# A new table of orders, engines and PSUM banks for a four-layer attention kernel on one core

## The chip, the core and the metric

The kernel runs on one core of a Trainium2 chip. A core has five engines that run side by side, each with its own instruction stream that it works off in order: TensorE (PE: matmuls, with its weight loads shown apart as PEld), VectorE (DVE), ScalarE (ACT), GpSimd (POOL), and SyncE (SP), which here only issues DMAs. PE writes its results to PSUM, a memory of eight banks per partition; DVE and ACT read them from there and write to SBUF, the working memory. The engines wait for each other by semaphores.

The metric is the device time of one execution in microseconds (us). Before the change it is 412.26 us, the median of three runs (411.99 to 412.7).

## The reference

The input x has 2048 rows (tokens) of 512 numbers in bf16. Four layers follow each other, each of the form x = x + attention(layernorm(x)), with 32 heads of 16 numbers: a linear attention (A), a sliding attention (B), A again and B again, with the same weights for both A and for both B.

```python
def _A_ref(x, wqkv, wo):            # linear attention
    phi = lambda t: jnp.where(t > 0, t + 1, jnp.exp(t)) + 1e-6
    pq, pk = phi(q), phi(k)
    kv = jnp.einsum("bhsd,bhse->bhde", pk, v)
    z = jnp.einsum("bhsd->bhd", pk)
    num = jnp.einsum("bhqd,bhde->bhqe", pq, kv)
    den = jnp.einsum("bhqd,bhd->bhq", pq, z)[..., None] + 1e-6
    o = num / den                   # then o @ wo
...
def _B_ref(x, wqkv, wo):            # each row sees itself and the 255 rows before it
    scores = jnp.einsum("bhqd,bhkd->bhqk", q, k) * (Dh ** -0.5)
    mask = (idx[:, None] - idx[None, :] >= 0) & (idx[:, None] - idx[None, :] < W)
    p = _softmax(jnp.where(mask[None, None], scores, -1e9), axis=-1)
    o = jnp.einsum("bhqk,bhkd->bhqd", p, v)     # then o @ wo
```

## The kernel before

**Tiles and stages.** The rows are cut into 16 tiles of 128. The program first builds a graph of 2559 operations (class Plan), each a small group of instructions on one engine, with what each must wait for. The stages are:

1. The first A layer's keys (layer_a_keys): for each tile a layer norm (norm: statistics L374 and L375 on DVE, two tiny steps L379 and L380 on POOL, the normalised tile L381 on DVE), a transpose of the tile (a DMA, L389, or PE with a copy, L395 and L402), key and query projections (tok L420, feat L434) and the function phi (exponential L444 on ACT, the rest L446 to L451 on ACT and DVE). A product of normalised input and keys is summed over all tiles (L501).
2. The barrier: the summed product becomes a small matrix M; denominators are formed (L563, L569) and spread (L579), and the queries are divided (L589, L591).
3. The first sliding layer (middle(2)). For each tile: the output of the A layer (tok L420), the residual (L604, DVE), a norm, a transpose, the B projections (feat L434, tok L420), and copies of their results out of PSUM: queries by "bqe" (L407), keys by "bke" (L627 on ACT, L628 on DVE) and values by "bve" (L407). A DMA spreads the keys ("kd", L636) and one the values ("vd", L655). Then the scores (L676, and L792 for the far end of the window), their exponentials "ex" on ACT (L686, L801), the masks of the near triangle on DVE (L694) and of the far triangle ("mf") on DVE (L773) or on POOL (L772), the product with the values (L822), the division (L834, L835), a transposing DMA (L389) and the output projection with its residual. As each tile ends, the next A layer's norm, keys and values (their copy is "ve", L407) are begun.
4. The second barrier, then the second sliding layer (middle(3)), whose finished tiles are sent to the output by DMAs ("outp", L942), issued by SP or POOL.

**Which operations have a choice.** Most operations are bound to one engine. Copies out of PSUM (made by copy, either and transpose) may run on ACT or on DVE; a far mask on DVE or POOL; an output DMA on SP or POOL.

**What sets the order.** Nothing is scheduled while the kernel is built. A packed string, TABLE (from L954), holds a decision for everything, and place (L92) reads it: two bytes for each of the 2559 places give the operation that stands there in one overall order; one byte for each operation gives its engine; one byte for each of the 1005 PSUM tiles gives its bank, 0 to 7. Each engine then runs its own operations in that overall order.

```python
order = [ops[raw[2 * k] + 256 * raw[2 * k + 1]] for k in range(n)]
o.eng = ("PE", "ACT", "DVE", "POOL", "SP")[raw[2 * n + o.i]]
x.banks = [raw[3 * n + k]]
```

Two waits follow from the table itself. A PSUM tile that takes over a bank waits until the tile that held the bank before has been read. And a long POOL operation (a far mask among them) is made to wait for the nearest short DVE operation (norm or mask) that stands before it in the overall order. synchronise (L133) turns all dependencies into semaphore waits; SP's DMAs use a ring of 48 semaphores.

Of the kernel before, what the change touches and what calls it, by code (L numbers as in the profile page):

```python
# [11 lines left out]
P = 128  # L12
D = 512
DH = 16
S = 2048
T = 16
# [219 lines left out]
class Plan:  # L236
# [715 lines left out]


TABLE = (  # L954
    r"c-qZZ1GH_+j;*AUO4YS(+qP}nwr$(CZQHhO+h*^z&%Lkz@5lf8{~o>0SxP0TnVDHN_6n(#3ZYPu0>vt{(khG!tBeY#;;UdPxccG}D67J&gzBTqtRkpSE~5J8",
    r"5~(cegG;Qksun7VilmaNY^tS-tg@?Cs*n2YqNp6IwMwQYsGKUfimLi5QE62hl|uDX(NtR%N~Ke|RXdeZEmn<GdevXmRuk0{HA!Vqb<_a0O)XUeRbACyrBahs",
    r"V>L)^R~^(cHAU4^JJeJaL)BLuRT{NZEmtvBF_lrRP@U9ZwM)fPomF&oOYK&%RYR3Y4N<q%3Ds5IQA1TX6;}mT2I8o@s=Lag;;Cuso@$~}tCMP&y050IH|msX",
    r"sv4-_YKA(kR;rn5l{%y5s#)r+TCEDIE=r(>daH`7HEN#9t0F*8wMPX~7J8`>s)SmrMk)ur)hP8&1%ml1BJ5SURA4BhvcMd*PmNZIV1b&g_N(_QE38usRV4VJ",
    r"&Zz_HqlygYRdrPi8o&khKqZDKkOYduLv>L_g>2AFtyh=SBb84bRF72<$PQ0bP$&VHRSpOSC84>>2~X7+6&yaPr0`jdQ)5*rIHbO)WY7?j!&emzzNxAzI$Tj9",
    r"pftpQ{OXyC2?}CC1(ge&8n1Fg5S0Q7sXUMp@<J#`1^J+`Dg$L9HGEfPRT>xvjUXhHgE$aW6;S0N9aMnvPyi}H5!D!KLu_aYwP2A-3sqEps0c+>JE#FQVS}ou",  # L960
    r"+Cv?v3-zF!st+BY2^?0Pp@wP$9iauZg;vlKHmWYr3|hkx)d`wIcX+Ojs;{mGOn|O%OihI2YLlw0UZ_d1SzT2x)k4^!CPO8)2(GCq&<&=-3D~L@!*$gYrol;=",
    r"4mZ>$SOV45W>^X{;1mEXgPCwsAuNZvumUvnf_bnKN~&2<Ud@Lsa2RT-*{}e%!V#DQ+n_g`hNG|@*1{{*57xnP*a0_TJ?w;4&<A$GYUm5MU=5rBf{?fYUaPZk",
    r"8%kqMbqxB$J=h4Lkl_K8!E+EAOR3OsAI`%wD2o>$47`BdP!9J%SO|l6VIMq)aBv6q!(NDm2Ounlhqn+8W8*srj~Ah|ii4NnJw(8`_y{h;6?g&%p*&uNhfo0{",
    r";sAII*B~)g#DQ=gli~$D1eLH3Cc%qX8RO$qsEY}3EY`ytFb)&q2e=NYaXfy6PmmVlVS4xs8K6FXfi!pttKdtxjIUq<W`rx49wT7}oQSXCDrSPnI0=(sReS>(",
    r"aWY21sE8O16Ja&X3=OdXCdcU52&>~YOo5GY3bw^eI2CJPI&6<AaUQ0^`B)R%p~mY-xB#0XV`glQ9WV<Te1OgHD+p%AhiEYyeurt82Opus>G%zrU`GsuG4Te@",
    r"z|MFR17i!U47acoDy#y4*)cEH#vGUrYhg>wiTSY=7Qh%-6&7O`j0;OKH_pUrFbiAb608onFbEdJpx6eN;c_g5!EiR-#+7&ngJWTg2SqRhuE3($74Kp<j1Q}D",
    r"J$A<guo@TPMob86um^6yemDr$;yN4*n{gp-#i39Pi{lX3f)VvFh@>}R34Dp$@HLji?N|zT;46%*zhV?!O@G7cdMEC}{`ehh=mYo^qv`=zQ$NROx*!b1Cs+ug",
    r">t`54_ryUMQzz1e;RVjtz3>gr(SxxFJkYgtQK+qZV`BXnhu~cOP$$ttu@8R4gZK%D;URpahhtwH4xjNb?nb5O;#=H<BcP7HkMD3Ve!)4ITG!R@5%dvEtM?=7",
    r"4_Hs9(T{a<y$@sQCtB;2I<_W#4@Y1e{Zt3iDfCE8r=RJ}dY&GIjdW6-MaR{naSX=OS@nE<6tnA8`WQCW@pTTJUN_Olae>aDbLxe<jb5ZP>iW8^&ZHaY6PQc4",
    r"(<iZmey#)SY`UTDsDtQaI=61GgX&J2bsil|8{J$7*Ligd-C2jwqVwq<x}`3nd+9aW>QmTLC(urx#>KjiK7(s@Kix&I(;;<h-BtJ1p>!*K7B}i{`W%MVn{`p$",  # L970
    r"T^G~+^(Nh0Z`H;10G&{8(<Ssky<L~o`SliEN)OV@byGc97tkwoY28dO(Pi{Xy+Ie$d-YPiUw_nv^)g*nf71K(NC=}x>QV4nht;DYoIa>u=&_KL4(ntTUXOu7",
    r"x|}|w*XsznyiQIP^bkEt57ia*OI=C7(!+EL8m)KellrwzNn>;?N=2u1YdWG+(@uRrpVnz;mmaRu(pZf&Lch^OZD_TAt9R?8dX*lhHMOPj`k3CM-{}eZtp29c",
    r"(Q&P4qFzrY^dx;oZ=mlw5N)LNbWR5*pp2A(GEop>`l5r;CNlIvhoGP&)Q;Zk%+#KOQ*QdI&+87<k@C_7ZE3Q06q54L6n#-=qwF+QU()%h6HU{h=&~+A)Abb{",
    r"nsU%pU64vs7|KasC@htwuT+R4Q$FfOW$2pjPTwdO6{o^fj!M#Xy_tGY5!yl}XaH@cqSTp+(LgFiUFbWNr$MB+D-EFvG?cc{4PB9L>S0ugYEU>jK(}-h3QxCn",
# [12 lines left out]
    r"gp}$MN-{}$$swVohD4Bvl1rvbO_?D%rHRaxVUk&z$#BUc;bnw0l{_+1vPxbVCAB1*jF#GxUGm8oDI#MflH``6GEO2(9Z6w|Nfb$Gl1hGQA*oDVDIo=<rKC0m",
    r"C5<UAt)zn_lR}c+6qZhs!<3Xs(oyP}dNNt+o5qsKOp!(=vuPwbO+(W~vX};@lysBQlFMW@xy^X#DifrP?30O-&CHSRvR~#&b2%@a<$@fLxza~2N)PEP2c@U<",
    r"lS49J7RX^~E#IV<ER^rkTaHK@IV#F7l4H`?tdJ(At*n%(lFoviC9C9$w3DdPUea5%S7os@vjauj)zaK%umj|ptdZH0(Jqm-(!wqkvZrL7uw5p`-jL;TT3Xs$",
    r"a$L^H3ArijWs9`3*JXp8lh$^doRp0+P1@M4@<1-jCJAmg%R}ieA?zTzBq8l187ybzi3}03&m@z*ErD!i+tyn9R31wf8^&g}fo(YJY&LsGo=aGJSAy6bvQr}1",  # L990
    r"d-6i=OGJCuyp%|GyVS9v?JLP|UrSvZ%0{*YY<Anu7PR&38wqc7*tfDvg4vvQx4e@$c8^4{L2X?7UiL~<`%ykfE*sBAvjc2yJIJ=Td29ze&_=g0Y)9MO#<V@`",
    r"Cy8Zy+9dX~<g>|aY}?6xk<K=$jc<$CE;fNJW(V7Zwy14t3fn|BvHdE|ObOfEl(O^eeA~jLv?c8VTftVcrR{ZF$hI`=ZC+c^F0_5@4ZFzpv&HQOyV%~eDQsW6",
    r"(N?jk>@8c>ma+Zq5?j_*vr}w2o7yh5Q|)bA-Y&Bd+#Q?7Ms(BcU0dDmv6XEkx7XINk=;H!#@@3vZE`!#F1NMp3R~NbwNYF{JHoECQQZ*Rz>c)5?0vi1j<P%K",
    r"8avePwDoOC*V|6FyX+R*%MP={Z7H|auC@E^c)QJZwMXn|+sKx7M{PGd!#1{M+&cTh9<v{9S=YqAwB_7q``Es+<=rQ{+n%t|+;%&`Hnk`11v}B6vYYKB`_>+}",
    r"lkF4x-p;h|>{IL90UOvwcL(ir8_2OcWMjAo_OKOq+CH>r>?Zrj8u!(Hu^;SN`_0a>=j?3z-JZ8W+$EdM&9Mnx4rg5=H`l(gF<o|-*u`?Mt#YYcZ1>EjcFA0F",
    r"7ssV=aa|gh&c$<=ZF(2VU9q)X1((5HwG~}1SKFm^*KA6c+ks2q>Ns?HTt*ktHFiN=Q>R@a7tA$r?Okw3E`;mgs=B-`r>o{J+K#TitL`efX0D;D=?c4{(!e!$",
    r"p<P+2>{_}^u8NEATDZ<Gv#a5{xO^_D%i^-SB(AG#<wm<kF25V&!nnGwfD7viy0NaFo9@E7nXZ!??!vonu85oA2D!m5tsUuBxgl<Z8}G)s)o!9|?bf&nu8o`R",
    r"+PYD$yPM-?xgM^ao9iaI&2E_M=_b2gZmXN;`noA@iQD4VyQyxP+u(+}`EHx*;}*D$uD9Fo*1CnRs5|Huxnk~s+wGRR;;x_D<2JeeZo6CT*0}+0ue<0DxgBnx",
# [168 lines left out]
```

## Time and profile before

| | |
|---|---|
| median of 3 runs | 412.26 us (411.99 to 412.7) |
| span of the profiled execution, first to last instruction | 410.8 us |
| granted TensorE clock | 1.000 |
| matmuls, weight loads | 7668, 7742 |
| DVE, ACT, POOL instructions | 807, 448, 216 |
| DMA traffic | 37.19 MB, most of it inside the chip; HBM read 6.29 MB, written 2.10 MB |

The profile is of one execution. Its span leaves out what lies before the first and after the last instruction; the median of the runs is 1.5 us above the span, and this difference is carried along unchanged in all sums. An engine's "busy" is the time in which at least one of its instructions runs. Matmul ends are modelled, so PE's busy share is not its share of useful work. A line like L420 is shared by several steps, since helpers record it.

### The profile page before, as it was taken

How to read it: one execution, taken by the hardware profiler on the slowest of the kernel's cores; microseconds unless marked ns; L12 is line 12 of the kernel's file. 1: busy time of each engine (PE TensorE's matmuls, PEld its weight loads, DVE VectorE, ACT ScalarE, POOL GpSimd, SP SyncE). 2: the span in 40 equal slices, each digit the busy share in tenths (PEclk: the TensorE clock that was granted, in tenths of full speed). 3: DMA queues.
4: the chain of work that ended last, by engine and by line, in shares of the span. 5: the costliest groups of instructions: out<-in, count | busy, mean ns of one | idle time of the engine just before them, and what ended most of it. 6: DMA issues, size and time to landing. Idle time of an engine off the chain costs nothing.

```text
span 410.8 us, 17540 instructions
## 1 busy us (share of the span) xinstructions
PE 386.9 (94%) x7668; PEld 260.3 (63%) x7742; DVE 344.5 (84%) x807; ACT 352.8 (86%) x448; POOL 122.4 (30%) x216
## 2 busy tenths in 40 slices
PE   7999999999999999999999999999999988999896
PEld 3654676766575576566567777586757755566674
DVE  6997799989998899888887789997899688857585
ACT  4654659998999999999998357999999999999993
POOL 4576653111252331320503203303113304303020
PEclk9999999999999999999999999999999999999999
DMA  7495114443243435353222100344314821561751
GB/s 249 101 217 144 49 34 115 120 70 90 56 106 74 119 77 107 81 119 82 68 41 57 27 2 2 105 109 81 102 44 122 122 66 41 120 127 56 168 107 42
DMA packets 66596, 37.19 MB, mean 91 GB/s; under 512 B 47640, under 2 KB 61848, under 8 KB 66520
## 3 DMA queue, kind: packets, MB, share of 16 engines
q1 hardware_dynamic: 66032, 34.75, 37.0%
q8 instruction: 61, 1.00, 1.1%
q0 software_dynamic: 480, 1.31, 1.0%
q14 instruction: 15, 0.12, 0.1%
q10 hardware_dynamic: 8, 0.00, 0.0%
HBM read 6.29 MB, written 2.10 MB: 20 GB/s over the span
## 4 chain that ended last, share of the span: by engine, by line
PE 51%; ACT 34%; DVE 9%; DMA 3%; issue 2%; SPq 1%; POOL 1%
ACT pb L686 20%; PE ps L420 18%; PE ps L434 10%; PE ps L822 10%; PE ps L676 5%; ACT pb L801 5%; ACT vp L686 4%; PE ps L501 3%; ACT tE L444 2%; DMA wA<-in_A_wqkv_dram 2%; DMA xT<-xn 1%; DVE xres L604 1%; DVE stats L374 1%; ACT pb L721 1%; PE ps L477 1%
## 5 line engine op out<-in xcount | busy, mean ns | idle before, releaser
L686 ACT ACTIVATE pb<-ps 128x1024 bf16<-128x1024 f32 (+2 forms) x216 | 198.9, 1020 | 5.2 <-PE ps L676 3.9
L822 PEld LDWEIGHTS ps<-vB,pb 128*128 128x128 bf16 x2560 | 77.7, 96 | 12.3 <-DVE pb L694 3.6
L822 PE MATMUL ps<-vB,pb 128*128 128x34 bf16 x2560 | 83.5, 177 | 0.6 <-POOL pb L772 0.3
L434 PE MATMUL ps<-xT,wBp 128*128 128x128 bf16 x1024 | 69.0, 219 | 1.7 <-ACT tE L444 0.6
L434 PEld LDWEIGHTS ps<-xT,wBp 128*128 128x128 bf16 x1024 | 58.5, 98 | 13.7 <-issue 4.4
L379 POOL TENSOR_SCALAR ve<-mv 128x1 f32<-128x1 f32 x63 | 16.7, 265 | 154.7 <-DVE mv L375 152.7
L444 ACT ACTIVATE tE<-ps 128x512 bf16<-128x512 f32 x64 | 38.6, 612 | 27.1 <-PE ps L420 11.2
L772 POOL TENSOR_SCALAR_AFFINE_SELECT pb<-pb 128x1024 bf16<-128x1024 bf16 x30 | 34.4, 1146 | 71.4 <-DVE pb L694 23.8
L676 PE MATMUL ps<-XQ,kB 32*128 32x256 bf16 (+3 forms) x992 | 48.0, 267 | 3.3 <-ACT pb L754 0.7
L604 DVE TENSOR_TENSOR xres<-ps,xres 128x512 bf16<-128x512 f32 x63 | 43.0, 684 | 6.7 <-PE ps L420 6.3
L420 PE MATMUL ps<-wA,XQ 128*128 128x512 bf16 x174 | 45.6, 379 | 2.2 <-issue 0.6
L374 DVE BATCH_NORM_STATS2 stats<-xres 128x6 f32<-128x512 bf16 x64 | 43.5, 685 | 2.8 <-DMA xres<-in_A_x_dram 2.2
L694 DVE TENSOR_TENSOR pb<-pb,tri 128x512 bf16<-128x512 bf16 (+1 forms) x108 | 41.5, 396 | 3.3 <-ACT pb L686 3.1
L801 ACT ACTIVATE pb<-ps 128x1024 bf16<-128x1024 f32 x42 | 41.4, 1059 | 1.1 <-PE ps L792 0.9
L380 POOL TENSOR_TENSOR rs<-ve,negh 128x1 f32<-128x1 f32 x64 | 37.8, 591 | 8.3 <-DVE ve L377 3.0
L434 PE MATMUL ps<-XQ,wA 128*128 128x128 bf16 x512 | 35.4, 219 | 0.3 <-DMA wA<-in_A_wqkv_dram 0.3
L434 PEld LDWEIGHTS ps<-XQ,wA 128*128 128x128 bf16 x512 | 30.7, 98 | 7.3 <-DMA wA<-in_A_wqkv_dram 0.8
L420 PE MATMUL ps<-wBv,xT 128*128 128x512 bf16 x110 | 31.4, 380 | 2.6 <-issue 1.0
L676 PEld LDWEIGHTS ps<-XQ,kB 32*128 32x128 bf16 x992 | 15.0, 92 | 29.5 <-ACT pb L686 7.5
L420 PE MATMUL ps<-M,XQ 128*128 128x512 bf16 x113 | 30.7, 380 | 2.3 <-ACT vp L686 0.4
L420 PE MATMUL ps<-wBo,oT 128*128 128x512 bf16 x105 | 28.8, 380 | 2.8 <-issue 1.0
L686 ACT ACTIVATE vp<-ps 128x1024 bf16<-128x1024 f32 (+2 forms) x32 | 26.7, 928 | 1.5 <-PE ps L676 1.5
(126 smaller groups left out, 551.6 us busy)
## 6 DMA issues: line engine op xcount, KB each, us to landing
vB<-vS SPq DMA_DIRECT2D x64, 136.0 KB, 2.7
kB<-vp SPq DMA_DIRECT2D x60, 128.0 KB, 2.3
wA<-in_A_wqkv_dram SPq DMA_DIRECT2D x3, 512.0 KB, 5.5
out_dram<-xres POOLq DMA_DIRECT2D x10, 128.0 KB, 2.8
xres<-in_A_x_dram SPq DMA_DIRECT2D x2, 512.0 KB, 5.1
pb<-in_B_wqkv_dram SPq DMA_DIRECT2D x1, 1024.0 KB, 5.8
xres<-in_A_x_dram SPq DMA_DIRECT2D x3, 256.0 KB, 5.5
out_dram<-xres SPq DMA_DIRECT2D x5, 128.0 KB, 2.7
```

Of the source, the lines that this page charges most:

```text
L374: self.on("DVE", "stats", lambda e: e.bn_stats(K.stats[:, t, :], x()), key, dve(512), rd=rd, wr=[("stats", t)], **held)
L380: self.pow = self.on("POOL", "pow", lambda e: e.tensor_tensor(K.rs[:, t, :], K.ve[:, t, :], K.negh[:], ALU.pow), key + 0.03, (640, 690), r ...
L420: m = e.matmul(K.ps(ps), lhs(c), rhs(c), start=c == 0 and not whole, stop=c == 3)
L434: m = e.matmul(K.ps(ps)[:, f * P:(f + 1) * P], w(c, f), xT(c), start=c == 0, stop=c == 3)
L444: self.on("ACT", "E", lambda e: e.activation(K.tE[:, s, :], K.ps(ps), ACT.Exp, bias=0.0), key, act(512), wr=[("tE", s)], ps=[ps])
L604: self.on("DVE", "res", lambda e: e.tensor_tensor(K.xres[:, t, :], K.ps(po), K.xres[:, t, :], ALU.add), key, dve(512), rd=[("xres", t)], w ...
L676: m = e.matmul(K.ps(ps[gq])[:, ns * i:ns * i + ns], K.kB[rows, j % 4, 2 * f + b, :, :], K.XQ[rows, f, q:q + ns], start=True, stop=True, ti ...
L686: return e.activation(out(2 * h, 2, ns), i, ACT.Exp, bias=0.0, scale=0.25)
L694: return e.tensor_tensor(x, x, K.tri[:, 0, sh:64].unsqueeze(1).unsqueeze(1).to_broadcast([P, 4, n, 64 - sh]), ALU.mult)
L772: return e.affine_select(out=x, in_=x, compare_op=ALU.is_ge, fill=0.0, base=-2, pattern=[[0, 16], [-2, 64]], channel_multiplier=1)
L801: return e.activation(far(h), i, ACT.Exp, bias=0.0, scale=0.25)
L822: m = e.matmul(K.ps(ps)[:, 34 * u:34 * u + 34], K.P((b // 2) % rp)[:, gq, f, o:o + P], K.vB[:, (b // 2) % 4, b % 2, r, :], start=i == 0, s ...
```

## The change

Only TABLE is replaced: 54 lines of packed text for 54 others. The graph, the instructions of each operation and both rules of place stay as they are.

```diff
@@ -952,60 +952,60 @@
 TABLE = (
-    r"c-qZZ1GH_+j;*AUO4YS(+qP}nwr$(CZQHhO+h*^z&%Lkz@5lf8{~o>0SxP0TnVDHN_6n(#3ZYPu0>vt{(khG!tBeY#;;UdPxccG}D67J&gzBTqtRkpSE~5J8",
...
+    r"c-qZb1+*nMj<qDqvYVOG%*@?MGcz+YbDEi%nVFfHnVFfHnIT*Celk0gWG0jB>^W2aysEM+U0+?R^nRVERCpCZMO3K5s8A}jN~992a4M2YqLQkxDzefli^{69",
...
 )
```

Unpacked with place's own layout, the two tables compare as follows. "#n" counts operations of one name in the order of the graph; the tile is given in brackets, and the times are those at which the operation begins in the profile of before.

**Engines.** 52 operations change engine.

| operations | from | to |
|---|---|---|
| far masks mf: 15 | DVE | POOL |
| far masks mf: 10 | POOL | DVE |
| output DMAs: 5 (tiles 0, 2, 3, 8, 11) | POOL | SP |
| output DMA: 1 (tile 5) | SP | POOL |
| PSUM copies: 14 | ACT | DVE |
| PSUM copies: 7 | DVE | ACT |

So far masks on POOL go from 33 to 38, and ACT has 440 graph operations in place of 447. The 21 copies, by stage of the profile of before:

- up to 62 us, to DVE: sc#1 (46.1), Me#1 (47.2), bqe#1 (tile 1, 61.2); to ACT: sc#3 (48.2).
- 62 to 219 us, to DVE: bqe#5 (tile 5, 79.3), bve#4 (tile 4, 83.8), bqe#11 (tile 11, 146.1), bke#10 (tile 11, 151.0), bve#11 (tile 11, 171.5), ve#2 (tile 7, 179.6); to ACT: bqe#12 (tile 12, 154.1). Far masks in this stage: six from DVE to POOL, three from POOL to DVE.
- 219 to 253 us, to DVE: ve#7 (232.1); to ACT: ve#13 (220.7), oTe#0 (229.1), ve#10 (238.4).
- 253 to 398 us, to DVE: bqe#18 (tile 2, 258.4), bke#18 (tile 4, 273.4), bqe#30 (tile 14, 368.0); to ACT: bve#16 (tile 0, 254.9), bqe#20 (tile 4, 270.7). Far masks: nine from DVE to POOL, six from POOL to DVE.
- after 398 us, to DVE: oTe#1 (403.2).

**Orders.** To turn the old order of an engine into the new one, so many of its operations at least have to move, counted over those that stay on the engine: PE 205 of 866, ACT 53 of 433, DVE 293 of 784, POOL 72 of 197, SP 92 of 227. No PE operation moves by more than 17 places among PE's, no ACT operation by more than 12 among ACT's, no DVE operation by more than 46. Among those that lie within 0 to 45 us, 44 of PE's 93 move; within 219 to 259 us 36 of 98; in the two sliding stages 63 of 333 and 44 of 282. SP's moves lie mostly in the sliding stages: 40 of 100 and 44 of 89.

**Banks.** 462 of the 1005 bytes that give the banks differ.

More of the change, by code (lines that the diff above doesn't have):

```diff
@@ L959 @@
[L959 to L974, printed above, removed]
```

90 lines of the change are left out of this document (53 added, 37 removed).

## The prediction

> **What bounds the kernel now.** The first view is the page: busy times of the engines, then the share of each engine in the chain of work that ended last.
>
> ```profile
> PE 386.9 (94%) x7668; PEld 260.3 (63%) x7742; DVE 344.5 (84%) x807; ACT 352.8 (86%) x448; POOL 122.4 (30%) x216
> PE 51%; ACT 34%; DVE 9%; DMA 3%; issue 2%; SPq 1%; POOL 1%
> ```
>
> No engine is alone at its limit over the whole span, so the second view cuts the span at the borders of the stages.
>
> ```profile
> 0.00:45.00 45.00, 42.17 (x352) 22.95 (x358) 36.73 (x98) 22.29 (x37) 27.37 (x63) 1.00 0.64 173
> 45.00:62.00 17.00, 16.58 (x234) 12.18 (x236) 16.01 (x36) 11.12 (x20) 8.98 (x17) 1.00 0.12 26
> 62.00:219.00 157.00, 150.02 (x3114) 99.47 (x3143) 139.23 (x322) 151.76 (x178) 41.70 (x70) 1.00 0.39 87
> 219.00:253.00 34.00, 33.22 (x565) 24.94 (x569) 28.09 (x67) 19.12 (x35) 8.41 (x14) 1.00 0.10 22
> 253.00:398.00 145.00, 135.88 (x3190) 94.14 (x3212) 117.13 (x270) 143.11 (x170) 34.38 (x53) 1.00 0.43 94
> 398.00:410.80 12.80, 8.98 (x237) 6.60 (x235) 7.33 (x19) 5.40 (x12) 1.62 (x3) 0.99 0.25 71
> ```
>
> The columns are the stretch, its length, then busy time and count of PE, PEld, DVE, ACT and POOL. The reader is to see that ACT works 22 of 45 us and 19 of 34 us in the A stages, but 151.76 of 157 and 143.11 of 145 us in the two sliding stages, three quarters of the span. There PE's 150.02 and 135.88 contain modelled ends. The third view asks what ended ACT's little idle time there (62 to 219 us, then 253 to 398 us):
>
> ```profile
> ACT pb L686 <- PE ps L676: 2.6, 6, 0.6
> ACT tE L444 <- PE ps L420: 0.6, 2, 0.4
> ACT pb L721 <- PE ps L712: 0.5, 1, 0.5
> ...
> ACT vp L686 <- PE ps L676: 0.6, 1, 0.6
> ACT pb L801 <- PE ps L792: 0.6, 1, 0.6
> ```
>
> So the sliding stages run at ACT's pace, with about 5.2 us of holes in the first (157 less 151.76) and 1.9 in the second. The chain by lines tempers this in the first sliding stage: PE lines lead there (L420, L822, L434), with ACT's L686 at a sixth. ACT and PE take turns, because each score group needs a bank that ACT has emptied and each value product needs ACT's exponentials.
>
> ```profile
> by line: PE ps L420 24.4%; ACT pb L686 16.5%; PE ps L822 14.7%; PE ps L434 13.9%; PE ps L676 8.1%; ACT pb L801 4.7%; issue 2.3%; ACT tE L444 2.1%; PE ps L792 1.6%; DVE stats L374 1.1%; DVE pb L694 1.1%; DVE xn L381 0.9%; DVE vS L407 0.9%; D
> ```
>
> **The change part by part.** No operation is added or removed, so a gain can come only from work taken off ACT where ACT sets the pace, or from holes that close.
>
> **1. Copies off ACT in the first sliding stage.** ACT's copies there, and how densely ACT repeats its exponentials:
>
> ```profile
> L407 ACT ACTIVATE vS<-ps 128x512 bf16<-128x512 f32 x5 | 3.6, 723 | 0.0
> ...
> L627 ACT ACTIVATE vp<-ps 128x512 bf16<-128x512 f32 x2 | 1.5, 772 | 0.0
> L407 ACT ACTIVATE XQ<-ps 128x512 bf16<-128x512 f32 x2 | 1.2, 603 | 0.0
> L407 ACT ACTIVATE vp<-ps 128x512 bf16<-128x512 f32 x1 | 0.7, 678 | 0.0
> ```
>
> ```profile
> 67.74 9.27 ACT L686 ACTIVATE pb<-ps 128x1024 bf16<-128x1024 f32 x10
> ```
>
> Six copies leave: two bqe (2 x 603 ns), two bve (2 x 723), one bke (772), one ve (678), together 4.10 us. One bqe enters (0.60). Net 3.50 us. Ten exponentials fill 9.27 us and a lone one takes 1.02, so each further one adds (9.27 - 1.02) / 9 = 0.92: successive ACT instructions overlap by 0.10 us. With five instructions fewer I take off 0.5: ACT's work falls by **3.0 us**.
>
> DVE takes them over:
>
> ```profile
> L407 DVE CAST vS<-ps 128x512 bf16<-128x512 f32 x26 | 18.0, 691 | 6.4 <-PE ps L420 5.9
> L628 DVE CAST vp<-ps 128x512 bf16<-128x512 f32 x23 | 16.8, 731 | 7.2 <-PE ps L434 6.7 <-DMA kB<-vp 0.3
> L407 DVE CAST XQ<-ps 128x512 bf16<-128x512 f32 x23 | 15.7, 685 | 3.4 <-PE ps L434 3.3
> L773 DVE TENSOR_TENSOR pb<-pb,tri 128x1024 bf16<-128x1024 bf16 x20 | 15.2, 766 | 0.1
> L772 POOL TENSOR_SCALAR_AFFINE_SELECT pb<-pb 128x1024 bf16<-128x1024 bf16 x30 | 34.4, 1146 | 71.4 <-DVE pb L694 23.8 <-ACT pb L801 15.0 <-DVE pb L773 12.3
> ```
>
> It gains five copies net (about 5 x 0.69 = 3.5 us) and gives three far masks net to POOL (3 x 0.766 = 2.3): 1.2 us more, 140.4 of some 154 us, 91%. That is cover enough on average, though a residual or mask queued behind a copy on DVE is late by up to 0.73 us, and PE's score group or value product after it too. POOL gets 3 x 1.15 = 3.4 us, of which it has plenty. The gain lies between 0 (PE or DVE takes over at once) and 3.0, or 8.2 with all holes closed; a loss isn't excluded (rivals). I take **-2.2 us**, near the ACT rows but short of them, since the chain shows PE in turn with ACT.
>
> **2. The same in the second sliding stage.** Two bqe and one bke leave; one bqe and one bve enter. By page rows of ACT in that stage, XQ 612, vp 787 and vS 712 ns (the last over the whole span):
>
> ```profile
> L627 ACT ACTIVATE vp<-ps 128x512 bf16<-128x512 f32 x4 | 3.1, 787 | 0.1
> L407 ACT ACTIVATE XQ<-ps 128x512 bf16<-128x512 f32 x5 | 3.1, 612 | 0.0
> ...
> L407 ACT ACTIVATE vS<-ps 128x512 bf16<-128x512 f32 x6 | 4.3, 712 | 0.0
> ```
>
> 2 x 0.612 + 0.787 - 0.612 - 0.712 = 0.69, less 0.1 of overlap: **-0.5 us**, bounds 0 and -0.6.
>
> **3. SP's queue and the holes of the second sliding stage.** SP issues in order, so a transpose that waits for its input holds back those behind it. The issues around ACT's hole at 324.6 us:
>
> ```profile
> 318.42 1.19 SPq L389 DMA_TRANSPOSE xT<-xn  x1
> 319.65 1.73 SPq L389 DMA_TRANSPOSE oT<-o  x1
> 321.67 1.18 SPq L655 DMA_DIRECT2D vB<-vS  x2
> 322.99 1.22 SPq L389 DMA_TRANSPOSE xT<-xn  x1
> ...
> 324.63 1.94 ACT L801 ACTIVATE pb<-ps 128x1024 bf16<-128x1024 f32 x2 [0.56 <-PE ps L792]
> ```
>
> In the new order this oT stands two places ahead of the first xT. Between 253 and 398 us half of SP's DMAs move. I let one of the two holes of 0.6 us close: **-0.6 us**, bounds -1.9 and, by the same row, +0.6 for each hole that opens. Four output DMAs net go from POOL to SP; at 1.18 us for two, SP's queue gets 4 x 0.59 = 2.4 us, spread over 100 us: nothing, except that transposes wait behind them by 0.6 each.
>
> **4. The A stages.** Up to 62 us and from 219 to 253 us PE is busy 58.75 of 62 and 33.22 of 34 us, and ACT isn't the limit, so the copies that change engine there cost nothing. The PE orders change much. What PE could still gain is what it idles, 3.2 and 0.8 us; a bad order costs as much. The start waits for DMAs in any order. I take 0 and **-0.5**. The 462 other banks: PE waits on ACT for a bank by rows like
>
> ```profile
> PEld ps L676 <- ACT pb L686: 7.5, 17, 0.8
> ```
>
> Bounds: -7.5 if all such waits went (ACT's pace would still remain), as much if they doubled. I take 0.
>
> **5. The end.** The last transposed tile but one is copied by DVE in place of ACT:
>
> ```profile
> L402 ACT ACTIVATE oT<-ps 128x512 bf16<-128x512 bf16 x1 | 0.6, 597 | 0.3 <-PE ps L395 0.3
> L402 DVE COPY oT<-ps 128x512 bf16<-128x512 bf16 x1 | 0.4, 425 | 0.3 <-PE ps L395 0.3
> ```
>
> 597 - 425 ns: at most **-0.2 us**; its like at 229 us goes the other way. I take -0.1.
>
> **6. More masks on POOL.** One such mask beside a far mask on DVE:
>
> ```profile
> 195.96 1.15 POOL L772 TENSOR_SCALAR_AFFINE_SELECT pb<-pb 128x1024 bf16<-128x1024 bf16 x1 [3.44 <-DVE xn L381]
> ...
> 196.40 1.24 DVE L773 TENSOR_TENSOR pb<-pb,tri 128x1024 bf16<-128x1024 bf16 x1
> L726 DVE TENSOR_TENSOR pb<-pb,tri 128x1024 bf16<-128x1024 bf16 x2 | 1.4, 676 | 0.0
> ```
>
> A product of the same shape takes 676 ns alone and 1.24 us here: 0.56 us lost. All 20 of L773 average 766, so the whole loss there is 20 x 0.09 = 1.8 us for 33 masks on POOL, 0.055 each. Five more: **+0.3 us**.
>
> The Trainium skill, "SBUF — State Buffer", section "Who interferes with whom", says that a DVE instruction with two SBUF inputs and a GpSimd instruction that reads SBUF exclude each other, and the later one waits for the whole of the earlier. The trace shows that such overlaps cost, with 1.24 against 0.68 us. By the rule alone every meeting costs up to the rest of a 1.15 us mask, and the sum would be that of the third rival, not +0.3.
>
> **Sum**: -2.2 - 0.5 - 0.6 - 0.5 - 0.1 + 0.3 = -3.6 us on a span of 410.8, which gives 407.2; with the 1.5 us around it, 412.3 - 3.6 = **408.7 us**.
>
> **The rivals.**
> - *The holes close as well.* If ACT's holes of 5.2 us in the first sliding stage half close (-2.6) and PE's 3.2 us before 62 us shrink by a third (-1.1): 405.0. For it: every one of these waits is a matter of order. Against it: PE is itself at 150 of 157 us.
> - *The relief is swallowed.* ACT has less to do, but PE leads the chain, and parts 1 to 3 come to nothing: 412.3 + 0.3 - 0.6 = 412.0. For it: the chain's shares above. Against it: PE's busy time there holds modelled ends, and ACT's holes are 3%.
> - *DVE and POOL exclude each other*, slower: 15 masks are new on POOL. Should each stop a DVE mask or norm for 0.56 us, DVE loses 8.4 us where it is 91% full, and value products wait: 412.3 - 3.9 + 8.4 = 416.8. It decides from the seventh such meeting on (3.9 / 0.56). Against it: 33 masks now cost 1.8 us in all.
> - *A late DMA in SP's queue*, slower: 84 of the 189 SP issues in the sliding stages move. Each transpose that waits ahead of another costs a hole like the 0.56 us one; ten of them give 412.3 - 3.6 + 5.6 = 414.3, and from the seventh on the kernel is slower. For it: DMA times vary, and no order knows them. Against it: from an A layer's output projection to the B projection that needs its transposed norm, never fewer than 19 PE operations lie between in the old order, 20 in the new; from a tile's last value product to its output projection 10 and 9.
>
> **How the numbers follow.** Forecast 0.52; closing holes 0.14; swallowed 0.12; exclusion 0.09; late DMAs 0.13. A measurement of this kernel can tell about 0.2% (0.8 us) from no change. Of the swallowed case 0.09 lies within that and 0.03 to the faster side; of the late DMAs 0.01 lies within. Faster: 0.52 + 0.14 + 0.03 = 0.69; same 0.10; slower 0.21. The range runs from 404.5, which leaves out little of the closing holes, to 414.0, which takes in the swallowed case and the milder part of the slower ones.
>
> **What would show it.** Right: ACT busy at most 149 us in the first sliding stage, that stage 2 to 3 us shorter, the second 1 us, the A stages within 1 us, L773's mean near 766 ns. Wrong: ACT's holes in the sliding stages beyond 9 us in all, with releasers PE L676 or L792 (late banks or DMAs); L773 or L694 well above 766 and 416 ns; or A stages that change by more than 1 us, which no row here could tell.

## The result, and the profile after

| | before | after |
|---|---|---|
| median of 20 runs each | 412.53 us (411.54 to 413.82) | 415.5 us (413.53 to 419.27) |
| ratio after / before, 95% interval | | 1.0073 [1.0056, 1.009] |
| span of the profiled execution | 410.8 us | 413.8 us |
| mean granted TensorE clock | 1.000 | 0.996 |

The kernel became slower by 3.0 us (2.3 to 3.7 by the interval). Forecast were 408.7 us, within 404.5 to 414.0: the sign is wrong and the time lies outside the range. First the page of after, busy times and shares of the chain:

```profile
PE 388.9 (94%) x7670; PEld 263.3 (64%) x7742; DVE 349.8 (85%) x809; ACT 349.4 (84%) x441; POOL 127.7 (31%) x217
PE 60%; ACT 22%; DVE 10%; issue 6%; POOL 1%; POOLq 0%
```

ACT has 3.4 us less to do (352.8 before), about what was forecast, and leads less of the chain (34% before, now 22%). DVE has 5.3 us more (344.5), of which what moves explains about 1: seven copies more (7 x 0.69) and five far masks fewer (5 x 0.77). The first two stretches of the prediction, same columns, in after:

```profile
0.00:45.00 45.00, 43.10 (x362) 23.81 (x367) 38.02 (x98) 21.78 (x37) 27.25 (x64) 1.00 0.59 161
45.00:62.00 17.00, 14.51 (x192) 9.89 (x193) 16.78 (x32) 9.28 (x16) 10.10 (x17) 0.95 0.05 10
```

Up to 45 us PE is no less busy than before (42.17). The second line is the one to look at: from 45 to 62 us PE is busy 14.51 us in place of 16.58, with 192 matmuls in place of 234, and its clock is 0.95. (Each of these two traces lacks some 70 of the 7742 matmul records, so PE's busy times are a little low in both.) Everything later starts late, so the windows of the two sliding stages are moved along by 4 and 3 us:

```profile
66.00:223.00 157.00, 149.27 (x3093) 100.03 (x3123) 139.98 (x324) 148.41 (x172) 43.60 (x69) 1.00 0.43 91
256.00:401.00 145.00, 136.76 (x3220) 95.22 (x3241) 118.08 (x268) 142.99 (x169) 37.24 (x52) 1.00 0.39 95
```

ACT, the fourth pair of numbers, has 3.4 us less than before in the first sliding stage (151.76) and as much in the second (143.11). To see where the time goes without windows that slip, compare equal sets of work. The two tables hold the same operations in their first 703 places (some 105 us) and in their first 1243 (188 us). "Late" is the end of the last matmul among the operations that stand in the first so many places of the old table, after less before, in the two profiled executions:

| places of the old table | 300 | 400 | 475 | 575 | 703 | 1243 | 1557 | all |
|---|---|---|---|---|---|---|---|---|
| end in before, us | 43.05 | 58.28 | 69.14 | 83.25 | 104.76 | 188.39 | 242.16 | 407.16 |
| after is late by, us | -0.2 | 2.2 | 3.2 | 4.3 | 3.9 | 3.6 | 3.4 | 3.1 |

The whole loss is made between the 43rd and the 83rd us of before: 3.2 us up to place 475, and 1.1 more up to place 575, to which run 5 returns. From place 703 to the end, where the forecast had nearly all its gain, the new table wins back 0.8 us.

The loss has a place. The stretches around it, and the idle time of PE in them, in after:

```profile
58.00:60.00 2.00, 0.41 (x16) 0.37 (x18) 2.00 (x4) 1.81 (x3) 0.26 (x1) 1.00 0.00 0
60.00:62.00 2.00, 1.92 (x7) 0.80 (x7) 2.00 (x5) 1.36 (x2) 0.58 (x2) 0.61 0.00 0
62.00:64.00 2.00, 2.00 (x23) 2.00 (x22) 2.00 (x5) 0.85 (x2) 0.21 (x1) 0.53 0.33 71
```

```profile
59.52 0.41 PE L579 MATMUL ps<-rec,spread 32*128 32x128 bf16 x16 [1.90 <-DVE XQ L451]
```

PE stands still for 1.90 us before 59.52 us, and from 60.45 to 63.86 us its granted clock is half. It waits for DVE, which is busy all the time. The chain from 52 to 62 us (start, us, what) tells what DVE does, and DVE's and POOL's timelines show why it takes so long:

```profile
54.40 0.80 DVE xn L381
55.20 2.18 DVE tE L447 x2
57.37 0.59 DVE XQ L451
57.97 0.86 DVE rec L569
58.83 0.56 DVE XQ L451
59.38 0.14 issue
59.52 0.41 PE ps L579 x16
```

```profile
54.31 0.88 DVE L381 TENSOR_SCALAR xn<-xres,mv,rs 128x512 bf16<-128x512 bf16 x1
55.12 2.25 DVE L447 TENSOR_SCALAR tE<-tE 128x512 bf16<-128x512 bf16 x2
57.29 0.67 DVE L451 SCALAR_TENSOR_TENSOR XQ<-ps,tE 128x512 bf16<-128x512 f32 x1
```

```profile
54.29 0.76 POOL L356 COPY wBp<-pb 128x512 bf16<-128x512 bf16 x1
55.11 0.97 POOL L361 MEMSET pb<- 128x1024 bf16 x1
56.14 1.08 POOL L907 MEMSET vp<- 128x1152 bf16 x1
57.28 0.98 POOL L361 MEMSET pb<- 128x1024 bf16 x1
```

Two short steps at L447 (they make A's feature map from an exponential, "E1") take 2.25 us. In before the three such steps between 53 and 62 us take 0.26 to 0.29 us each. POOL sets one-off constants at the very moment: a fill from 55.11 to 56.08, the next from 56.14 to 57.22. The first E1 (1.11 us) ends just after the first fill, the second (1.22 us) just after the second. The norm step at 54.31 runs beside POOL's weight copy and takes 0.88 where one alone takes 0.41. Over the whole execution the same step grew from the first row (before) to the second (after):

```profile
L447 DVE TENSOR_SCALAR tE<-tE 128x512 bf16<-128x512 bf16 x64 | 18.0, 290 | 4.9 <-ACT tE L444 4.4
```

```profile
L447 DVE TENSOR_SCALAR tE<-tE 128x512 bf16<-128x512 bf16 x64 | 21.0, 334 | 3.8 <-ACT tE L444 3.5
```

3.0 us for the same 64 steps. Added up over all DVE steps, the time above the median of their kind is about 3.2 us in before and 6.5 in after.

The Trainium skill, "SBUF — State Buffer", section "Who interferes with whom", says that a DVE tensor_scalar can run in a mode with two ports, and then it and a GpSimd instruction block each other for a whole instruction, the later one waiting. The trace agrees: 0.28 us became about 1.1 beside each fill.

Why does it happen in the new table? place makes a long POOL operation (a fill or a weight copy too) wait for the nearest short DVE operation ahead of it in the overall list. In the old table, 24 long POOL operations of the first 703 places wait for 18 different short DVE steps. In the new one 25 wait for only 6, 16 of them for the same E1. The new list no longer runs in the order of time: operations of one engine stand in groups, so "nearest ahead" is often long past when POOL's turn comes, and POOL runs its fills in a row, beside whatever DVE does.

### The profile page after: what moved, and what is told of

The parts are those of the page before. It is cut to its first block, busy times and chain, and to the rows that moved or that the text cites. A ratio compares the mean times of both kernels' runs of the same rounds, so it can differ in the third digit from the quotient of the medians.

```text
span 413.8 us, 17514 instructions
## 1 busy us (share of the span) xinstructions
PE 388.9 (94%) x7670; PEld 263.3 (64%) x7742; DVE 349.8 (85%) x809; ACT 349.4 (84%) x441; POOL 127.7 (31%) x217
## 4 chain that ended last, share of the span: by engine, by line
PE 60%; ACT 22%; DVE 10%; issue 6%; POOL 1%; POOLq 0%
PE ps L420 20%; PE ps L434 15%; ACT pb L686 11%; PE ps L822 10%; PE ps L676 6%; ACT vp L686 4%; ACT pb L801 3%; PE ps L501 2%; DVE tE L447 2%; DVE vp L451 1%; ACT tE L444 1%; PE ps L792 1%; PE ps L1082 1%; DVE stats L374 1%; PE ps L477 1%
## 5 line engine op out<-in xcount | busy, mean ns | idle before, releaser
L434 PEld LDWEIGHTS ps<-xT,wBp 128*128 128x128 bf16 x1024 | 59.6, 99 | 12.2 <-issue 4.9
L379 POOL TENSOR_SCALAR ve<-mv 128x1 f32<-128x1 f32 x63 | 15.5, 246 | 160.3 <-DVE mv L375 158.6
L772 POOL TENSOR_SCALAR_AFFINE_SELECT pb<-pb 128x1024 bf16<-128x1024 bf16 x34 | 39.0, 1147 | 82.4 <-DVE pb L694 42.4
L676 PE MATMUL ps<-XQ,kB 32*128 32x256 bf16 (+3 forms) x992 | 48.3, 267 | 2.7 <-DVE o L835 0.7
L694 DVE TENSOR_TENSOR pb<-pb,tri 128x512 bf16<-128x512 bf16 (+1 forms) x108 | 42.0, 401 | 2.9 <-ACT pb L686 2.5
L380 POOL TENSOR_TENSOR rs<-ve,negh 128x1 f32<-128x1 f32 x64 | 40.3, 629 | 7.4 <-DVE ve L377 2.2
L420 PE MATMUL ps<-wBo,oT 128*128 128x512 bf16 x108 | 29.8, 380 | 3.6 <-issue 1.9
L676 PEld LDWEIGHTS ps<-XQ,kB 32*128 32x128 bf16 x992 | 15.3, 92 | 25.9 <-ACT pb L686 9.2
L834 DVE RECIPROCAL rc<-ps 128x16 f32<-128x16 f32 x64 | 16.2, 253 | 14.1 <-PE ps L822 13.9
```

Source lines behind the costliest of these rows:

```text
L380: self.pow = self.on("POOL", "pow", lambda e: e.tensor_tensor(K.rs[:, t, :], K.ve[:, t, :], K.negh[:], ALU.pow), key + 0.03, (640, 690), r ...
L420: m = e.matmul(K.ps(ps), lhs(c), rhs(c), start=c == 0 and not whole, stop=c == 3)
L434: m = e.matmul(K.ps(ps)[:, f * P:(f + 1) * P], w(c, f), xT(c), start=c == 0, stop=c == 3)
L676: m = e.matmul(K.ps(ps[gq])[:, ns * i:ns * i + ns], K.kB[rows, j % 4, 2 * f + b, :, :], K.XQ[rows, f, q:q + ns], start=True, stop=True, ti ...
L694: return e.tensor_tensor(x, x, K.tri[:, 0, sh:64].unsqueeze(1).unsqueeze(1).to_broadcast([P, 4, n, 64 - sh]), ALU.mult)
L772: return e.affine_select(out=x, in_=x, compare_op=ALU.is_ge, fill=0.0, base=-2, pattern=[[0, 16], [-2, 64]], channel_multiplier=1)
```

## The experiments

**Theory:** the loss comes from the first 62 us, where POOL's fills now meet short DVE steps, which opens a PE hole and halves the clock; the later orders give almost nothing. (Run 5 leads to a second, smaller source.) **Rivals:** the copies and masks that change engine cost it; or the clock alone does. Each time stands beside a before that was measured along with it (412.4, 412.2, 412.55 or 412.7 us).

**1. Where it is.** The new table with the first 703 places (order, engines, banks) of the old one; new_first is the reverse.

```diff
-    order = [ops[raw[2 * k] + 256 * raw[2 * k + 1]] for k in range(n)]
...
+    for upto, which in [(703, 0), (2559, 1)]:
+        for o in listed[which][:upto]:
+            if o.i not in of:
+                of[o.i] = tables[which]
+                order.append(o)
...
```

> The first 703 places of the table are those of before, the other 1856 those of the changed kernel. In the two profiles the changed kernel is 3.9 us late at this cut (last matmul of the first part at 108.69 against 104.76 us) and 2.9 to 3.1 us late at the end. Theory 1, all of the loss is made in the first part (POOL's fills stop DVE at 54 to 57 us, PE runs dry for 1.9 us, its clock is halved for 3.4 us): the rest keeps its gain of about 1 us, so 411.4 us against 412.5, ratio 0.996 to 0.999. Rival 2, the loss is spread over the later parts (late DMAs, masks on POOL) and the late first part only hides it: 413.5 or more, ratio above 1.002.

> The reverse: the first 703 places of the changed kernel, the rest of before. Theory 1: all of the loss and none of the later gain, 415.9 to 416.7 us, ratio 1.008 to 1.010, with a stretch of halved clock near 60 us in most runs. Rival 2: 412.5 to 413.5, ratio under 1.003.

Measured: old_first 411.57 us, ratio 0.9988 [0.9976, 1.0]; new_first 416.93, 1.0119 [1.0099, 1.0139]. So nearly all that the forecast counted on, from 105 us to the end, is worth 0.5 us (0 to 1.0), and the first part costs more than the whole loss. The profile of new_first shows the same hole as after, and a second one that waits for a DMA; the clock is half for 3.41 us after each:

```profile
54.82 2.25 DVE L453 TENSOR_SCALAR tE<-tE 128x512 bf16<-128x512 bf16 x2
```

```profile
59.22 0.49 PE L585 MATMUL ps<-rec,spread 32*128 32x128 bf16 x16 [1.90 <-DVE XQ L457]
...
86.56 0.89 PE L426 MATMUL ps<-wBo,oT 128*128 128x512 bf16 x2 [1.50 <-DMA oT<-o]
```

(Lines of edited kernels are shifted by a few.) Up to place 475 new_first is as late as after (2.9 and 3.2 us); the second hole takes it to 5.9 at place 575, where after has 4.3. But this profile is of the slowest of its five runs (418.74 us, mean clock 0.992). The other four show 0.996, which is one stretch at half, so the second stretch doesn't explain their times. Why the median loses 4.9 us, where the difference of after and old_first leaves 3.5 for the first part, stays open. old_first has the lowest time of all versions, though its interval reaches 1.0.

**2. The meeting itself.** The changed kernel, with one weight copy moved behind an E1 and three fills behind the last E1 of the stage; nothing else.

```diff
...
+    for what, behind in [(('wp', 4), ('E1', 13)), (('c24', 1), ('E1', 19)), (('zero', 1), ('E1', 19)), (('c24', 2), ('E1', 19))]:
+        o = one(*what)
+        order.remove(o)
+        order.insert(order.index(one(*behind)) + 1, o)
```

> The changed kernel with four POOL operations moved in the order: one weight permutation goes from 54.3 us to behind a short DVE step at 50.8 us, and three fills of memory (two of pb, one of vp) go behind the last short DVE step before the second reciprocal, so that they begin when DVE has done with it. Theory 1: the three DVE steps lose their 2.2 us of extra length (0.89, 1.11 and 1.22 us against 0.40, 0.29 and 0.28), PE's hole of 1.9 us shrinks to under 0.5, the clock stays full, and the time falls by 3 to 4 us to 411.5 to 412.5, ratio to before 0.997 to 1.000. Rival 2: within 0.8 us of the changed kernel's 415.5.

Measured: 412.75 us, 1.0007 [0.9993, 1.0022]. Four moved POOL operations take back 2.75 of the 3.0 us. The clock is full, and the three things hang together:

```profile
45.00:62.00 17.00, 16.67 (x251) 12.15 (x250) 16.67 (x36) 10.76 (x19) 10.90 (x19) 1.00 0.08 18
```

```profile
55.11 0.40 DVE L387 TENSOR_SCALAR xn<-xres,mv,rs 128x512 bf16<-128x512 bf16 x1
55.43 0.48 DVE L453 TENSOR_SCALAR tE<-tE 128x512 bf16<-128x512 bf16 x2
```

```profile
55.98 0.95 POOL L367 MEMSET pb<- 128x1024 bf16 x1 [0.95 <-DVE tE L453]
```

The first fill begins as the E1 pair ends; the pair takes 0.48 us in place of 2.25, and PE is busy 16.67 of 17 us.

**3. Hole or clock?** The changed kernel with six matmuls of 512 columns, whose result nobody reads, in PE's hole.

```diff
+            spreads = []
...
                     if o.name == "spread" and name == "PE":
+                        spreads.append(o)
+                        if len(spreads) == 2:
+                            e.wait_ge(sems["DVE"], 121)
+                            for _ in range(6):
+                                e.matmul(self.PS[:, 0, :], self.wBv[:, 0, 0:P], self.wBv[:, 1, :], start=True, stop=True)
```

> The changed kernel with six needless 512-column matmuls in PE's hole at 58 to 59.5 us, into a PSUM bank that is overwritten afterwards; the hole stays as long for all useful work. If the hole brings about the halved clock (theory 1), no stretch of halved clock follows, and 1.5 of the loss goes: 413.8 to 414.4 us, all runs at clock 1.0. If the clock falls for another reason, the halved stretch stays and the time stays within 0.8 us of 415.5.

Measured: 415.04 us, 1.0061 [1.0042, 1.0079]; the clock was full in all six runs, with the meeting as before and the hole filled:

```profile
54.89 2.25 DVE L447 TENSOR_SCALAR tE<-tE 128x512 bf16<-128x512 bf16 x2
```

```profile
57.80 1.47 PE L1093 MATMUL ps<-wBv 128*128 128x512 bf16 x6 [0.40 <-DVE XQ L451]
```

So the hole is what halves the clock here. (Eight of the 20 runs of after have a full mean clock, 0.999 or 1.0, too; at that rate six in a row would come by chance once in some 240 times.) The clock came out as theory 1 has it, but the time lies in the range expected of the other case, so the clock's price was put too high. It is known only roughly. By the medians it is 0.5 us (415.5 to 415.04), with intervals that overlap widely. In the two profiles after is 3.2 us late at place 475 and filled_hole 1.5; at the end they are 3.1 and 2.3 us late. And the eight runs of after with a full clock have a median of 414.3 us, the twelve others 415.7, which is 1.4 us, though what else differs between them isn't known. So the half clock costs some 0.5 to 1.4 of the 3.0 us. The larger part, 1.8 us even in the runs with a full clock, is work that is late and stays late.

**4. POOL's places alone.** If those places were the whole cause, they could be exchanged between the tables: pool_as_before is the changed kernel with its 39 one-off POOL operations behind the same DVE steps as in the old table; pool_as_after is before with the places of the new one.

```diff
+    for k, o in enumerate(once):
+        p = order.index(behind[o]) + 1 if behind[o] else 0
+        p = max([p] + [order.index(d) + 1 for d in o.deps if d in order])
+        ...
+        order.insert(p, o)
```

> The changed kernel, but POOL's 39 operations that are made once (constants, fills, weight permutations) stand at the places of the old table, counted from DVE's operations; all else as changed. In the old table 24 long POOL operations of the first part wait for 18 different short DVE steps, in the changed one 25 for 6. If that is the whole cause of the first part's loss, the time comes to that of old_first, 411.6 (within 0.7 us); if the other new orders of the first part cost too, it stays near pool_late's 412.8 or above.

> The reverse: the kernel before with only these POOL operations at the places of the changed table. If POOL's places alone make the loss, DVE's short steps between 30 and 58 us are stretched by 2 us or more in all and the time rises by 2 to 4 us: 414.2 to 416.2. If the loss needs the new orders of the other engines too, under 1 us more.

Measured: pool_as_before 420.12 us, 1.02 [1.0174, 1.0227]; pool_as_after 418.29, 1.0144 [1.0127, 1.0161]. The first is far from what was expected: POOL runs in order, and its first weight copy now stands ahead of things that PE needs, waiting for a load. The waits from 30 to 62 us (us in total, times, longest) and the PE hole, first of pool_as_before, then of pool_as_after:

```profile
POOL wBp L380 <- DMA pb<-in_B_wqkv_dram: 7.1, 1, 7.1
...
DVE zs L568 <- POOL hot L362: 5.5, 1, 5.5
```

```profile
47.19 0.30 PE L587 MATMUL ps<-ones,eps 128*32 128x128 bf16 x4 [3.73 <-DVE zs L568]
```

```profile
DVE xn L405 <- POOL rs L404: 4.0, 1, 4.0
```

```profile
58.33 0.40 PE L419 MATMUL ps<-ident,xn 128*128 128x128 bf16 x4 [3.20 <-DVE xn L405]
```

pool_as_after shows a loss, but mostly by another wait: a norm's power on POOL stands behind the row of one-off operations. Neither run separates the meeting from the queue; run 2 does.

**5. All of POOL's row.** After run 2, steps before 50 us were still stretched by 1.8 us in all (three E1 by 0.4 each and one product by 0.5), against 0.5 in before. Is that the 1.2 us which separates pool_late from old_first? The changed kernel, with POOL's row cut into groups behind six different E1.

```diff
+SPREAD = [
+    (('E1', 20), [('c21', 1)]),
+    (('E1', 24), [('zero', 0)]),
...
+    (('E1', 19), [('c21', 0), ('c22', 0), ('c24', 0), ('c24', 2), ('zero', 1), ('c24', 1)]),
+]
```

> The changed kernel with POOL's run of one-off operations broken up: a fill or constant each behind a short DVE step, the long run only where DVE has no short step for 5 us, and five fills behind the last short step before the second reciprocal. If the stretched steps (0.42, 0.45, 0.38 and 0.51 us between 33 and 47 us) make what is left of the first part's loss, the time falls from pool_late's 412.8 by about 1 us to 411.6 to 412.0, and their stretch is gone in the trace. If the new orders themselves cost it, it stays within 0.5 us of 412.8.

Measured: 415.26 us, 1.0058 [1.0037, 1.008]; the expectation missed. The hole at 58 us is gone, and DVE is stretched by 3.75 us in place of 6.5. But six fills in a row behind the last E1 keep POOL busy from 56.0 to 61.5, and the next norm stands behind them:

```profile
61.62 0.22 POOL L399 TENSOR_SCALAR ve<-mv 128x1 f32<-128x1 f32 x1 [0.16 <-POOL pb L381]
```

```profile
62.53 0.41 DVE L401 TENSOR_SCALAR xn<-xres,mv,rs 128x512 bf16<-128x512 bf16 x1 [1.53 <-POOL rs L400]
```

```profile
64.19 1.04 PE L440 MATMUL ps<-M,XQ 128*128 128x512 bf16 x4 [0.99 <-DVE XQ L611]
```

In pool_late the same step on POOL starts at 59.89 and the norm at 60.89. So a POOL operation has two prices: meet a short DVE step, or hold up a norm. This kernel loses a further 1.6 us between place 703 and the end, where it has after's table. Its profile, of the slowest of its six runs (416.51 us), has a PE hole of 1.21 us there, at 161.12 us, that waits for a late transposing DMA (XQ from xn); whether the other runs have it isn't known.

Where the 1.2 us goes can be read from the traces, by the same measure of "late": pool_late is 0.4 us late at place 475 and 1.7 at place 575. Between the two lies a PE hole that waits for a DMA. The load of B's output weights (wBo, 512 KB) stands 25th in SP's queue in before, and 43rd in the new table, two places ahead of the first DMA that transposes an attention output (oT). First before's load; then load, transpose and PE's hole in after; then the hole in pool_late:

```profile
39.69 0.37 SPq L302 DMA_DIRECT2D wBo<-in_B_wo_dram  x1
```

```profile
79.97 0.61 SPq L302 DMA_DIRECT2D wBo<-in_B_wo_dram  x1
...
81.23 2.59 SPq L389 DMA_TRANSPOSE oT<-o  x1
```

```profile
86.31 0.38 PE L420 MATMUL ps<-wBo,oT 128*128 128x512 bf16 x1 [0.92 <-issue]
```

```profile
83.48 0.59 PE L426 MATMUL ps<-wBo,oT 128*128 128x512 bf16 x2 [0.92 <-DMA oT<-o]
```

In after this oT lands 4.77 us after its issue, at 86.00 us (2.42 us in before), and the first output projection starts right behind it. All six kernels with the late load show the same: oT takes 4.5 to 5.6 us, and they lose 0.8 to 3.1 us between places 475 and 575. In the ten with the early load it takes 2.4 to 3.1 us, and those without extra work there lose 0.2 at most. The load alone was not moved in any run, so this cause is read from the traces and not shown by an experiment.

**6. The engine choices alone.** The seven copies of the first sliding stage (part 1) changed in before, in its own order; the nine far masks of that stage alone; and both.

```diff
+SWAPPED = {("bqe", 5), ("bve", 4), ("bqe", 11), ("bke", 10), ("bve", 11), ("ve", 2), ("bqe", 12)}
...
+        if (o.name, k) in SWAPPED:
+            o.eng = {"ACT": "DVE", "DVE": "ACT"}[o.eng]
```

> The kernel before, with its own orders and banks; only the seven copies of the first sliding stage get the engines of the changed table (six from ACT to DVE, one from DVE to ACT). If ACT sets the pace there, as the prediction's first part had it, 3.0 us less work on ACT give 1.5 to 3 us: 409.4 to 410.9, ratio 0.993 to 0.997. If PE sets it (rival), ACT gets longer holes, with PE's scores as their releaser, and the time stays within 0.6 us of 412.4.

> The kernel before with only the nine changed far masks of the first sliding stage (six to POOL, three to DVE): 2.3 us less on DVE. If each engine's work is worth about 0.75 us per us in both directions, as adding it showed (2.8 for 3.6 on DVE, 2.9 for 3.5 on ACT), the time falls by 1.7 us: 410.5. If a relief isn't worth what a load costs, within 0.6 us of 412.3.

> The kernel before with the seven copies and the nine far masks of the first sliding stage, all in the old orders. By the slopes that adding work showed: ACT 3.0 us less, DVE 1.2 us more, -2.2 + 0.9 = -1.3 us, so 411.0. If a relief isn't worth what a load costs: between 412.3 and 414.2, the time of the copies alone.

Measured: copies_only 414.15 us, 1.0041 [1.0022, 1.006]; masks_only 413.02, 1.0004 [0.9984, 1.0023]; copies_masks 415.6, 1.0082 [1.0068, 1.0096]. Copies and masks together lose 3.4 us, twice what the copies lose alone; why isn't shown. The losses of copies_only and copies_masks lie outside both times that were expected of each. copies_only, 62 to 219 us, and what ACT waits for there:

```profile
62.00:219.00 157.00, 152.43 (x3093) 98.26 (x3092) 139.97 (x322) 147.65 (x170) 41.43 (x70) 1.00 0.38 86
```

```profile
ACT pb L692 <- PE ps L682: 6.6, 11, 1.0
```

ACT is busy 4.1 us less in this stretch (151.76 in before), part of it because work slips out of the stretch; over the whole execution it is 2.3 us less (352.8 and 350.5). Yet the kernel lost 1.7 us. The relief turned into a wait: ACT's exponentials wait 6.6 us for scores that PE makes late, in place of 2.6. The masks cost nothing that can be told.

**7. The price of work on each engine.** In before, needless work spread over the first sliding stage: seven exponentials on ACT (about 3.5 us), six statistics on DVE (3.6 us), sixteen matmuls on PE (3.5 us, some 13 of them in this stage).

```diff
...
+                if first and h == 0 and j % 2:
+                    i = K.ps(ps[0]).rearrange("p (f b n) -> p f b n", f=4, b=2)
+                    e.activation(K.pqd[:].rearrange("p f (b n) -> p f b n", b=2), i, ACT.Exp, bias=0.0, scale=0.25)
...
+            if again:
+                e.bn_stats(K.spare[:, t, :], x())
...
+                if twice and h == 0:
+                    e.matmul(K.ps(ps), lhs(0), rhs(0), start=True, stop=True)
```

> The kernel before, with seven needless 512-column exponentials on ACT in the first sliding stage, one in every second tile, into memory that nobody reads at that time: some 7 x 0.5 = 3.5 us more work on ACT. If ACT sets the pace, 3 to 3.5 us more: 415.4 to 416. If PE does, under 1.5 us more.

> The kernel before, with six needless statistics steps on DVE in the first sliding stage, 6 x 0.6 = 3.6 us more work on DVE, results unused. If ACT or PE sets the pace, under 1 us more, since DVE is busy for 139 of 157 us. If DVE is the engine that swallows the relief of ACT (it took over the copies), 2 us or more.

> The kernel before, with one needless 512-column matmul in each of the 16 value projections of the first sliding layer, whose result is overwritten: 16 x 0.216 = 3.5 us more work on PE, of which some 13 lie in the first sliding stage (2.8 us). If ACT sets the pace, under 1 us more. If PE does, 2.5 to 3.5 us more: 415 to 416.

Measured: act_more 415.28 us, 1.0063 [1.0044, 1.0082]; dve_more 415.16, 1.0075 [1.0046, 1.0104]; pe_more 416.59, 1.0099 [1.0066, 1.0132]. By the ratios +2.6, +3.1 and +4.1 us, 0.74, 0.86 and 1.2 for each us added. These prices are rough: the intervals run from 1.8 to 3.4, from 1.9 to 4.3 and from 2.7 to 5.4 us. None of the three has slack that swallows work; "91% busy" was no cover for DVE.

**8. Do the new later orders need their engines?** old_first, with all the PSUM copies behind place 703 that change engine back on the engines of the old table.

```diff
+COPIES = ("bqe", "bke", "bve", "ve", "oTe")
...
-        o.eng = ("PE", "ACT", "DVE", "POOL", "SP")[of[o.i][2 * n + o.i]]
+        o.eng = ("PE", "ACT", "DVE", "POOL", "SP")[(tables[0] if o.name in COPIES else of[o.i])[2 * n + o.i]]
```

This turns 15 copies back, nine of them to ACT.

> The old first part with the new later parts (old_first, 411.6), but all PSUM copies of the later parts on the engines of the old table. If the relief of ACT is what gains there, the gain of 0.8 us turns into a loss of 1 us or more: 413 or above. If the new orders gain by themselves, within 0.6 us of 411.6.

Measured: 421.77 us, 1.0219 [1.0198, 1.024]: 10.2 us above old_first, while ACT's busy time differs by 2.1 us (353.1 and 351.0). PE waits for an ACT copy ahead of a score group, and in the profile the clock is half for 3.41 us from 185.1 (the mean clock is below 0.999 in two of the five runs, so that isn't what makes the 10 us):

```profile
184.83 0.44 PE L685 MATMUL ps<-XQ,kB 32*128 32x256 bf16 x8 [1.24 <-ACT vp L416]
```

New engines in the old order cost 1.7 us, old engines in the new order 10. So as far as these runs go, orders and engines are one choice, and neither has a price without the other.

## Why the prediction was wrong, by its own steps

- **Part 4, the first A stage, is the step that failed** ("I take 0"). It put the new order of the first stages at nothing, and named PE's idle time there, 3.2 us, as the most that a bad order could cost. Measured by difference: 3.0 us for the whole change and -0.5 for what lies behind place 703 leave 3.5 us for the first part; run 2 ties 2.75 of them to four POOL operations, and the late load of wBo adds some 1.1 in the traces (run 5). The idle time that is there bounds what an order can win, not what it can lose: the 1.90 us hole and the half clock behind it are new. Nor were the 3.2 us all idle, since before's trace lacks 74 matmul records. In old_first, which has the same first places and no record missing, PE idles 1.9 us before 62 us (43.20 and 16.87 us busy), 1.25 of them before its first matmul. And even the bound that was written down did not get into the range: swallowed relief (412.0) with those 3.2 us would have been 415.2, where the range stopped at 414.0.
- **The third rival named the mechanism** (DVE and POOL exclude each other) and gave it 0.09, but for the wrong operations. It counted meetings with far masks. Those became milder at L773 and hardly changed at L694, as the groups of after show (their means were 766 and 416 ns in before):

```profile
L773 DVE TENSOR_TENSOR pb<-pb,tri 128x1024 bf16<-128x1024 bf16 x16 | 10.8, 679 | 0.4
L694 DVE TENSOR_TENSOR pb<-pb,tri 128x512 bf16<-128x512 bf16 x92 | 38.0, 422 | 2.1 <-ACT pb L686 1.6
```

  So part 6 (+0.3) doesn't show: by its own account the loss at L773 fell from 1.8 us to almost nothing, and run 6 finds no price for the masks. The fills and weight copies of the first stages weren't counted at all, though place's rule treats them as it treats masks.
- **Part 1 (-2.2) was right for ACT and mis-sized for the kernel.** ACT's busy time fell by 3.4 us to 148.41, below the 149 asked for. But from place 703 to 1557, which holds most of the stage, only 0.5 us came back (3.9 us late, then 3.4), not 2 to 3. For this part of the kernel the swallowed relief (412.0, given 0.12) was the right account: old_first takes 411.57. Run 6 shows the relief turn into ACT's wait for PE, and run 7 that 3.5 us more on DVE cost about as much (3.0) as 3.5 us on ACT (2.6). That accounts for a relief that is worth nothing, but not for the whole loss of copies_only. In after, from 66 to 223 us:

```profile
ACT pb L686 <- PE ps L676: 5.6, 11, 0.7
PEld ps L676 <- ACT pb L686: 4.7, 11, 0.4
```

  In before these waits were 2.6 and 3.0 us (62 to 219 us): both grew, each engine waits longer for the other, and the step "cover enough on average" failed.
- **Parts 2, 3 and 5 (-1.2 in all)** can be had only together: 0.3 us from place 1557 to the end. ACT's holes in the second sliding stage are 2.0 us (145 less 142.99) after 1.9, so none closed on balance; which of the parts brought the 0.3 isn't shown. Part 4's second half (-0.5, 219 to 253 us) wasn't tried alone.
- **The signs of being wrong that were named in advance came:** ACT's holes in the sliding stages are 8.6 + 2.0 = 10.6 us, beyond the 9 set, with releaser PE L676, and an A stage changed by more than 1 us.
- **The rival with SP's queue** (given 0.13) came true once, for some 1.1 us, but in another form than it gave: not a transpose behind another transpose, but a transpose behind a 512 KB load of weights (run 5). Against this rival the prediction counted PE's operations between a tile's last value product and its output projection (10 and 9); what SP issues just ahead of the transpose wasn't counted. The banks weren't tried by themselves.

## What to carry to other kernels

When only the order changes, look at what the slowest-moving engine (here POOL) now runs beside, one-off constants included: a rule that ties a wait to the nearest neighbour in a list protects only as long as the list runs in the order of time. Look at the DMA queue in the same way: a large load that moves back to its first use can make a small transfer behind it late. An engine that led the chain gave nothing back here when its work moved to another that was 90% busy; price a us on each engine before summing, and carry every "costs as much" bound into the range. An order is fitted to its engine choices, so a half of such a change tells little about the whole.

## What the runs showed of the hardware

- A PE hole far shorter than 3.41 us can be enough for half a clock. Idle times of 1.24 (copies_back), 1.50 (new_first), 1.90 (after, new_first) and 3.20 us (pool_as_after) were each followed by 3.41 us at half; one of 3.73 us (pool_as_before) went with 6.83. But six holes of 1.12 to 1.54 us in the same and other traces were not followed by it (the longest at 141.35 us in act_more, two of 1.43 and 1.46 us in copies_back), and none of 0.99 us or less was, nor the 1.90 us hole with needless matmuls in it. So between 1.1 and 1.6 us the length alone doesn't decide, and what does isn't shown. The Trainium skill, "TensorE: Matmul & The Clock Gate", section "HAM oscillation — how this bites in real kernels", gives as its rule no idle gaps above about 3.4 us; here gaps of 1.24 to 1.90 us were followed by the half clock too, so the measurement decides.
- A POOL fill, which reads nothing, stretched a DVE step of 0.28 us to 1.1 us, and two fills in a row caught two steps in a row.
- In this kernel 3.41 us at half clock cost 0.5 us by the medians of run 3 and 1.4 between the runs of after with and without it; in the profiles 1.6 us at place 475, of which 0.9 is left at the end.
- In six kernels a transposing DMA that was issued behind a 512 KB load took 4.5 to 5.6 us to land, in ten others 2.4 to 3.1.
